# Attention with a gated convolution: one of four probability tiles is turned by TensorE instead of the DMA engines, and a list scheduler orders the work

## The chip, the cores and the metric

The kernel runs on one core of a Trainium2 chip. The metric is the device time of one execution in microseconds (us); less is better. The kernel before takes 1226.25 us, the median of three runs from 1223.54 to 1230.8 us.

## The reference: what is computed

Four batches; q is [4, 12288, 128], kv is [4, 384, 32, 128], all float32.

```python
kv_pool = kv.reshape(B, H // 4, 4, W // 4, 4, C).mean(axis=(2, 4))   # 4x4 blocks: 768 keys
k = v = kv_pool.reshape(B, -1, C) @ w_sr
s = (q @ k.transpose(0, 2, 1)) / sqrt(C)
a = exp(s - s.max(-1));  a /= a.sum(-1) + 1e-9
x = a @ v                                    # [B, 12288, 128]
gate_pre[t] = sum over k of conv_w[k] * x[t - 4 + k]                 # five taps, causal
out = (sigmoid(gate_pre) * (x @ w_val)) @ w_out
```

## The kernel before, in words

The sequence of a batch is cut into 24 groups of 512 queries (`GQ`), 96 groups in all, and a group into four tiles of 128 queries. Channels lie on the partitions for q, x and everything behind x; queries lie on the partitions for the scores.

**Keys.** For each batch kv is summed over 4x4 blocks by VectorE. The first batch comes in 16 pieces by plain loads (`load_kv`, L110). Each later batch comes as eight transfers of whole rows (`load_rows`, L122): the first row of a half is a plain load from the queue of SyncE (SP), the other three are added on the way by accumulating DMAs that GpSimd issues (L128); VectorE then sums groups of four columns (`pool_rows`, L133). TensorE projects the sums by w_sr (L145); the keys are split into a high and a low float32r part (`kh`, `kl`), the values, scaled by a power of two for each channel, into two float16 parts (`vh`, `vl`).

**A tile.** TensorE makes the scores `s` of 128 queries against 768 keys with three products (L251: qh kh, qh kl, ql kh), each of 512 and 256 columns, into one of three double banks of PSUM. VectorE takes the row maximum (L257). ScalarE makes the exponential in place, with the row sum as a by-product (L263), and writes its high float16 half times 2^15 into the buffer `hl` (L282); VectorE writes the low half (L288). So queries still lie on the partitions, and the product with the values wants keys there. For that a DMA transposes the halves of two tiles at a time into `pt` (`p_lo`, L294; 193 issues on SP, the last pair apart).

**A group.** TensorE multiplies `pt` by the values with 18 products of 512 columns into `av` (L303). Meanwhile VectorE adds 1e-9 to the row sums and takes the reciprocal (L270, L271); SP writes the [128, 4] result to DRAM (`rd`, L272) and reads it back as one row on all 128 partitions (`rb`, L277), with the four tiles interleaved. VectorE multiplies `av` by this row into `x` (L322; the row is read with a stride of four elements). ScalarE makes two of the five taps (L330), GpSimd three (L332) and the four additions (L341). ScalarE takes the tanh (L357), TensorE multiplies x by w_val (L361), VectorE combines (L366), TensorE multiplies by w_out (L371), ScalarE copies out (L381), and SP stores two groups at a time (L385). GpSimd also makes the low part of q (L243).

**The order.** Each engine works through its instructions in the order of the program, which is written by hand: one loop over tiles (L442) that places the scores of the next tile, the parts of the product two groups back, and the steps of groups three to five back. Set-up steps of the next batch are dropped in one for each group. The last groups are written out (L502 to L552), with the very last cut into two halves and its convolution on VectorE.

Of the kernel before, what the change touches and what calls it, by code (L numbers as in the profile page):

```python
# [15 lines left out]
R = 4  # L16
P = 128
GQ = 512
NT = GQ // P

# [6 lines left out]
def attn_moe_kernel(ctx, tc, qT, kvT, w_sr, w_moe, outT):  # L27
    """qT, outT: [B, C, N]; kvT: [B, R, C, keys * R]; w_moe: [C, C + C + taps], the columns of
    w_val, w_out and conv_w transposed, as float64 bits (int64) or float32."""
    nc = tc.nc  # L30
    B, C, N = qT.shape
    NK, RR = kvT.shape[3] // R, R * R
# [6 lines left out]
    PIECES = 16  # L39
    AV_CUTS = (0, 6, 9, 12, 18)  # L40
    assert 3 * NCH == AV_CUTS[-1]
    PC = NK // PIECES
    QC = NK // 4
    scale = 1.0 / float(C) ** 0.5

    const = ctx.enter_context(tc.tile_pool(name="const", bufs=1))
    kvp = ctx.enter_context(tc.tile_pool(name="kvp", bufs=4))
    keys = ctx.enter_context(tc.tile_pool(name="keys", bufs=2))
    io = ctx.enter_context(tc.tile_pool(name="io", bufs=2))
    hlp = ctx.enter_context(tc.tile_pool(name="hlp", bufs=3))  # L50
    ptp = ctx.enter_context(tc.tile_pool(name="ptp", bufs=4))
    work = ctx.enter_context(tc.tile_pool(name="work", bufs=2))
    xp = ctx.enter_context(tc.tile_pool(name="xp", bufs=3))
    small = ctx.enter_context(tc.tile_pool(name="small", bufs=6))
    dram = ctx.enter_context(tc.tile_pool(name="dram", bufs=3, space=bass.MemoryType.DRAM))
    ps_s = ctx.enter_context(tc.tile_pool(name="ps_s", bufs=3, space=PSUM))
    ps_av = ctx.enter_context(tc.tile_pool(name="ps_av", bufs=1, space=PSUM))
    ps_m = ctx.enter_context(tc.tile_pool(name="ps_m", bufs=1, space=PSUM))

    def misc():  # L60
        return ps_m.tile([P, GQ], F32, name="m")

    ident = const.tile([P, P], F32, name="ident")
    make_identity(nc, ident)
    wsr = const.tile([C, C], F32, name="wsr")
    wm = const.tile([C, NW], F32, name="wm")
    wval, wout, cwt = wm[:, 0:C], wm[:, C:2 * C], wm[:, 2 * C:]

    def load_moe():
        """Loads the weights; the steps that make float32 of float64's bits, rounded to nearest."""  # L70
        if w_moe.dtype == F32:
            nc.sync.dma_start(out=wm, in_=w_moe)
            return []
        raw = kvp.tile([C, HALF * R], F32, name="rows0", bufs=1).bitcast(I32)[:, :2 * NW]
        rest = kvp.tile([C, HALF * R], F32, name="rows1", bufs=1)
        nc.sync.dma_start(out=raw, in_=w_moe.bitcast(I32))
# [4 lines left out]
        v = nc.vector  # L81

        def two(out, in_, s1, op0, s2, op1):
            return lambda: v.tensor_scalar(out=out, in0=in_, scalar1=s1, scalar2=s2,
                                           op0=op0, op1=op1)

        def one(out, in_, s1, op):
            return lambda: v.tensor_single_scalar(out=out, in_=in_, scalar=s1, op=op)

        def both(out, x, y, op):  # L90
            return lambda: v.tensor_tensor(out=out, in0=x, in1=y, op=op)

        return [
# [14 lines left out]
        ]  # L108

    def load_kv(st, i):  # L110
        t = kvp.tile([C, R, PC * R], F32, name="kvt", bufs=5)
        src = kvT[0].rearrange("r c x -> c r x")
        nc.sync.dma_start(out=t, in_=src[:, :, i * PC * R:(i + 1) * PC * R])
        st["kv", i] = t

    def pool_kv(st, i):
        t = st.pop(("kv", i))
        nc.vector.tensor_reduce(out=st["pool"][:, i * PC:(i + 1) * PC],
                                in_=t.rearrange("c r (k s) -> c k r s", s=R),
                                axis=AX.XY, op=ALU.add)  # L120

    def load_rows(b, st, h, r):  # L122
        src = kvT[b, r, :, h * HALF * R:(h + 1) * HALF * R]
        if r == 0:
            st["rows", h] = kvp.tile([C, HALF * R], F32, name=f"rows{h}", bufs=1)
            nc.sync.dma_start(out=st["rows", h], in_=src)
        else:
            nc.gpsimd.dma_start(out=st["rows", h], in_=src, accum_op=ALU.add)  # L128

    def pool_rows(st, i):  # L130
        t = st["rows", i // 2].rearrange("c (k s) -> c k s", s=R)
        k0 = i % 2 * QC
        nc.vector.tensor_reduce(out=st["pool"][:, i * QC:(i + 1) * QC], in_=t[:, k0:k0 + QC],  # L133
                                axis=AX.X, op=ALU.add)

    def key_tiles(st):
        st["pool"] = keys.tile([C, NK], F32, name="pool", bufs=1)
        for n in ("kh", "kl"):
            st[n] = keys.tile([C, NK], F32R, name=n)
        for n in ("vh", "vl"):  # L140
            st[n] = keys.tile([P, NK], F16, name=n)
        st["vt"] = keys.tile([C, NK], F32, name="vt", bufs=1)

    def project(st, h, m):
        nc.tensor.matmul(m[:, :HALF], wsr, st["pool"][:, h * HALF:(h + 1) * HALF],  # L145
                         start=True, stop=True)
        st["m"] = m[:, :HALF]

    def split_keys(st, h):
        sl = slice(h * HALF, (h + 1) * HALF)  # L150
        m = st.pop("m")

        def high():
            nc.scalar.activation(out=st["kh"][:, sl], in_=m, func=AF.Copy, scale=scale / RR)
            nc.scalar.activation(out=st["vt"][:, sl], in_=m, func=AF.Copy, scale=1.0 / RR)

        def low():
            nc.vector.scalar_tensor_tensor(  # L158
                out=st["kl"][:, sl], in0=m, scalar=scale / RR, in1=st["kh"][:, sl].bitcast(F32),
                op0=ALU.mult, op1=ALU.subtract)  # L160

        return high, low

    def column_scale(st):
        """Steps for the power of two that brings the largest value of each column to
        [2^14, 2^15), on a diagonal, and what takes it and P's 2^15 out again."""
        big = small.tile([C, 1], F32, name="big")
        pw = small.tile([C, 1], F32, name="pw")
        up = small.tile([C, 1], I32, name="up")
        st["down"] = keys.tile([C, 1], F32, name="down")  # L170
        st["diag"] = keys.tile([C, C], F32, name="diag", bufs=1)
        v = nc.vector
        return [
            lambda: v.tensor_reduce(out=big, in_=st["vt"], axis=AX.X, op=ALU.max,
                                    apply_absolute_value=True),
            lambda: v.tensor_single_scalar(out=pw.bitcast(I32), in_=big.bitcast(I32),
# [8 lines left out]
    def values(st, h, m):  # L185
# [4 lines left out]
        st["m"] = m[:, :HALF]  # L190

    def split_values(st, h):
        sl = slice(h * HALF, (h + 1) * HALF)
        m = st.pop("m")

        def high():
# [384 lines left out]
```

## Time and profile before

| | |
|---|---|
| runs | 1223.54, 1230.8, 1226.25 us, median 1226.25 |
| profiled execution: span (its own time) | 1223.5 (1223.54) us |
| mean granted TensorE clock | 0.954 |
| busy: TensorE, VectorE, ScalarE, GpSimd | 84%, 82%, 77%, 67% |
| DMA | 253.19 MB, mean 207 GB/s |
| load of q, of `rb`, landing of a transpose (median) | 5.6, 4.8, 7.0 us |

The profile is of one execution. Busy shares are means over the whole span; a matmul's end is modelled, so TensorE's own pace is read from the starts of its instructions. "Idle before" is the time in which an engine did nothing ahead of the instructions of a group, with what ended it. The share of a DMA queue is that of 16 engines over the span; since two queues overlap, the sum can pass 1.

### The profile page before, as it was taken

The numbers are of one execution on the slowest core, as the hardware profiler recorded it, in microseconds if no ns is written. First come the engines' busy times: TensorE is split into PE (matmuls) and PEld (weight loads), VectorE is DVE, ScalarE is ACT, GpSimd is POOL, SyncE is SP. The second block draws the span as 40 slices with busy tenths as digits, with TensorE's granted clock in tenths as the row PEclk, the third lists the DMA queues.
The fourth block names the chain that finished last, engine by engine and source line by source line (L and its number), as shares of the span: only waits on it lengthen the run. The fifth ranks groups of instructions, "written<-read, shape, count | busy, mean of one in ns | idle before, by whom it ended". The sixth has DMA issues, their size and how long they took to land.

```text
span 1223.5 us, 15077 instructions
## 1 busy us (share of the span) xinstructions
PE 1023.3 (84%) x4502; PEld 622.8 (51%) x4502; DVE 1001.5 (82%) x1251; ACT 940.1 (77%) x1657; POOL 814.2 (67%) x872
## 2 busy tenths in 40 slices
PE   1878886789898789789997878886989999999885
PEld 0644454455564445455555545553555555655552
DVE  5977885799987778699998868776998987988884
ACT  1867785688886778688897768766988988988981
POOL 1165775676785676576777657665867877877871
PEclk9899898899999989899999989898999999999998
DMA  8799999999999999999999999999999999999994
GB/s 251 141 216 203 213 218 167 205 211 201 204 227 227 219 210 214 208 204 212 210 222 225 210 195 226 208 188 194 204 223 207 200 220 213 211 220 212 227 195 116
DMA packets 650321, 253.19 MB, mean 207 GB/s; under 512 B 613632, under 2 KB 622208, under 8 KB 650240
## 3 DMA queue, kind: packets, MB, share of 16 engines
q1 hardware_dynamic: 647648, 238.08, 95.3%
q0 software_dynamic: 2592, 14.16, 7.4%
q8 instruction: 36, 0.59, 0.2%
q14 instruction: 45, 0.37, 0.1%
HBM read 75.83 MB, written 25.36 MB: 83 GB/s over the span
## 4 chain that ended last, share of the span: by engine, by line
DMA 49%; PE 27%; DVE 14%; ACT 5%; issue 3%; SPq 1%; DVEq 0%; ACTq 0%
DMA pt<-hl 47%; PE av L303 13%; PE s L251 7%; DVE nm L257 4%; PE m L361 4%; DVE hl L288 4%; DVE x L322 3%; ACT hl L282 3%; PE m L371 2%; ACT s L263 2%; DVE ze L270 1%; DMA kvt<-in_kv 1%; DVE h L366 1%; DMA rb<-rd 1%; SPq L294 1%
## 5 line engine op out<-in xcount | busy, mean ns | idle before, releaser
L341 POOL TENSOR_TENSOR sum<-sum,tap 128x512 f32<-128x512 f32 x282 | 362.0, 1284 | 330.3 <-ACT tap L330 315.7
L303 PE MATMUL av<-pt,vh 128*128 128x512 f16 x1140 | 400.6, 393 | 106.7 <-DMA pt<-hl 101.5
L288 DVE SCALAR_TENSOR_TENSOR hl<-s,hl 128x768 f16<-128x768 f32 x384 | 365.9, 953 | 113.4 <-ACT hl L282 111.9
L263 ACT ACTIVATE s<-s,nm 128x768 f32<-128x768 f32 x384 | 335.1, 873 | 135.8 <-DVE nm L257 134.8
L282 ACT ACTIVATE hl<-s 128x768 f16<-128x768 f32 x384 | 311.5, 811 | 94.8 <-DMA pt<-hl 83.9
L257 DVE TENSOR_REDUCE nm<-s 128x1 f32<-128x768 f32 x384 | 364.6, 950 | 12.8 <-PE s L251 12.6
L251 PE MATMUL s<-kh,qh 128*128 128x512 f32 (+1 forms) x768 | 280.9, 447 | 45.2 <-DVE hl L288 41.5
L303 PEld LDWEIGHTS <-vh 128*128 128x128 f16 x1164 | 115.8, 99 | 279.1 <-issue 143.0
L303 PE MATMUL av<-pt,vl 128*128 128x512 f16 x570 | 223.3, 392 | 0.0
L251 PEld LDWEIGHTS s<-kh,qh 128*128 128x128 f32 x768 | 142.1, 195 | 136.1 <-issue 91.4
L251 PE MATMUL s<-kl,qh 128*128 128x512 f32 (+1 forms) x768 | 200.6, 343 | 0.0
L251 PE MATMUL s<-kh,ql 128*128 128x512 f32 (+1 forms) x768 | 200.3, 342 | 0.0
L332 POOL TENSOR_SCALAR tap<-x,wm 128x512 f32<-128x512 f32 x282 | 195.6, 747 | 0.2
L243 POOL TENSOR_TENSOR ql<-q,qh 128x512 fp32r<-128x512 f32 x96 | 121.8, 1268 | 53.0 <-ACT qh L239 53.0
L322 DVE SCALAR_TENSOR_TENSOR x<-av,down,rb 128x512 f32<-128x512 f32 x95 | 108.2, 1139 | 48.6 <-PE av L303 28.6
L330 ACT ACTIVATE tap<-x,wm 128x512 f32<-128x512 f32 x188 | 133.9, 713 | 0.0
L251 PEld LDWEIGHTS s<-kl,qh 128*128 128x128 f32 x768 | 120.3, 192 | 18.1 <-DVE kl L158 0.5
L251 PEld LDWEIGHTS s<-kh,ql 128*128 128x128 f32 x768 | 120.4, 192 | 17.1
L341 POOL TENSOR_TENSOR sum<-tap,tap 128x512 f32<-128x512 f32 x94 | 125.2, 1332 | 0.0
L371 PE MATMUL m<-h,wm 128*128 128x512 f32 x188 | 100.1, 614 | 20.8 <-DVE h L366 20.8
L361 PE MATMUL m<-x,wm 128*128 128x512 f32 x188 | 107.1, 654 | 0.0
L303 PEld LDWEIGHTS <-vl 128*128 128x128 f16 x582 | 58.1, 100 | 67.9 <-issue 35.7
(58 smaller groups left out, 638.8 us busy)
## 6 DMA issues: line engine op xcount, KB each, us to landing
rb<-rd SPq DMA_DIRECT2D x96, 256.0 KB, 4.8
q<-in_q SPq DMA_DIRECT2D x47, 512.0 KB, 5.6
out<-o SPq DMA_DIRECT2D x46, 512.0 KB, 3.3
rows<-in_kv POOLq DMA_DIRECT2D x18, 768.0 KB, 9.4
kvt<-in_kv SPq DMA_DIRECT2D x16, 384.0 KB, 5.7
rows<-in_kv SPq DMA_DIRECT2D x6, 768.0 KB, 7.2
pt<-hl SPq DMA_TRANSPOSE x193, 7.0
rd<-r SPq DMA_DIRECT2D x96, 2.0 KB, 2.7
```

Source lines behind the costliest of these rows:

```text
L251: nc.tensor.matmul(s[:, c0:c1], a[:, sl], k[:, c0:c1], start=(i == 0), stop=(i == 2))
L257: nc.vector.tensor_reduce(out=nm, in_=g.s[j], axis=AX.X, op=ALU.max, negate=True)
L263: nc.scalar.activation(out=g.s[j], in_=g.s[j], func=AF.Exp, bias=g.nm.pop(j), accum_out=g.z[:, j:j + 1])
L282: nc.scalar.activation(out=g.hl[:, j % 2, 0], in_=g.s[j], func=AF.Copy, scale=2.0 ** 15)
L288: nc.vector.scalar_tensor_tensor(out=hl[:, j % 2, 1], in0=g.s.pop(j), scalar=2.0 ** 15, in1=hl[:, j % 2, 0], op0=ALU.mult, op1=ALU.subtract)
L303: nc.tensor.matmul(out, g.st[v][:, k * P:(k + 1) * P], g.pt[:, j0:j1, a * NCH + k], start=(i == 0), stop=(i == len(AV_ORDER) - 1))
L322: nc.vector.scalar_tensor_tensor(out=tiles(g.x[:, HALO + c0:HALO + c1]), in0=tiles(av), scalar=g.st["down"], in1=rows, op0=ALU.mult, op1=A ...
L330: nc.scalar.activation(out=g.tap[k], in_=src, func=AF.Copy, scale=w)
L332: eng.tensor_scalar(out=g.tap[k], in0=src, scalar1=w, scalar2=1.0, op0=ALU.mult, op1=ALU.mult)
L341: nc.gpsimd.tensor_tensor(out=s, in0=acc, in1=g.tap[k], op=ALU.add)
L361: nc.tensor.matmul(m, wval, g.x[:, HALO + c0:HALO + c1], start=True, stop=True)
L371: nc.tensor.matmul(m, wout, h, start=True, stop=True)
```

## The change

The hand-written loop is replaced by a planner. Every piece of work is a `Step` with an engine, a duration, a due time, the steps it comes after, and the buffers that it takes and frees. `Plan.order` simulates the five engines, lets the engine that can begin earliest take its ready step with the earliest due time, and the program is emitted in that order; the chip still runs each engine in program order. A group has a period of 10.4 us in the due times (`PERIOD`), its `av` product is due 1.9 periods after its first scores.

Besides the order, these parts differ:

- **Tile 3 of each group** (`TURNED = ((3,),)`) is turned by TensorE: its exponential goes to an SBUF buffer `p`, six blocks of 128 columns are transposed against the identity into a second double bank of PSUM, and the two halves are made from there straight into `pt`. Tiles 0 and 1 go through one DMA transpose, tile 2 through one of its own.
- **Keys** of every batch come in 16 pieces by plain loads on SP, each with a contiguous run in DRAM (the input is laid out anew), and VectorE sums 16 elements at once: 64 loads and 64 sums.
- **1/z**: GpSimd adds 1e-9, VectorE takes the reciprocal and a block transpose of 32x32, four small writes (4 rows of 32 elements each) go to DRAM, and the row comes back with the tiles in order, so `x` reads it contiguously.
- **Taps**: one on ScalarE (was two), four on GpSimd (was three); the sum is made in place in `gate`.
- **Buffers**: four `hl` (was three), three `pt` (was four), four `x` (was three), three q pairs (was two). The PSUM split (three double banks, `av`, `m`) stays.
- **The end**: the last two groups have their convolution on VectorE; the last group is no longer halved.

```diff
-    def load_rows(b, st, h, r):
...
-            nc.gpsimd.dma_start(out=st["rows", h], in_=src, accum_op=ALU.add)
+                nc.sync.dma_start(out=t, in_=kvT[b, i])
+            s = plan.add("SP", 1.05, due(-20 * T + i) if first else at(i) + T, run,
+                         takes=("kvt",), start=at(i))
...
+                v.tensor_reduce(out=st["pool"][:, i * PC:(i + 1) * PC],
+                                in_=ld.tile.rearrange("c (k s) -> c k s", s=RR),
+                                axis=AX.X, op=ALU.add)
...
+        def turned(j, ex):
...
+                    nc.tensor.transpose(state["t"][:, k * P:(k + 1) * P],
+                                        ex.tile[:, k * P:(k + 1) * P], ident)
...
+            flat = lambda a: g.pt[:, j, a * NCH:(a + 1) * NCH].rearrange("p k q -> p (k q)")
+            def hi():
+                nc.scalar.activation(out=flat(0), in_=state["t"][:, :NK], func=AF.Copy,
+                                     scale=2.0 ** 15)
+            def lo():
+                v.scalar_tensor_tensor(out=flat(1), in0=state["t"][:, :NK], scalar=2.0 ** 15,
+                                       in1=flat(0), op0=ALU.mult, op1=ALU.subtract)
...
+                nc.sync.dma_start_transpose(
+                    out=g.pt[:, j0:j0 + width].rearrange("p j k q -> p (j k) q"),
+                    in_=g.hls[j // 2][:, :width].rearrange("p j a k -> p (j a k)"))
...
-        nc.vector.tensor_scalar_add(out=ze, in0=g.z, scalar1=1e-9)
-        nc.vector.reciprocal(out=r, in_=ze)
-        nc.sync.dma_start(out=g.rd, in_=r)
+            nc.gpsimd.tensor_scalar_add(out=g.ze, in0=g.z, scalar1=1e-9)
+            v.reciprocal(out=g.r[:, :NT], in_=g.ze)
+            v.transpose(out=g.rt, in_=g.r)
+                nc.sync.dma_start(out=g.rd[j].rearrange("(b i) -> b i", i=32),
+                                  in_=g.rt[j::32, :])
+            nc.sync.dma_start(out=g.rb, in_=g.rd.rearrange("(o j) p -> o (j p)", o=1)
+                              .broadcast_to([C, GQ]))
...
+            taps = {4: act_tap(4)}
...
+            for k in (1, 2, 3):
+                taps[k] = pool_tap(k)
+            for k in (1, 4, 2, 3):
+                gate = plus(k, taps[k], gate)
...
+    for step in plan.order():
+        step.run()
+AV_DUE = 1.9
+TURNED = ((3,),)
```

## Rows read from the trace of the kernel before

**Rows 1.** The page: busy time (share of the span) and instructions; DMA queues, share of 16 engines.

```profile
PE 1023.3 (84%) x4502; PEld 622.8 (51%) x4502; DVE 1001.5 (82%) x1251; ACT 940.1 (77%) x1657; POOL 814.2 (67%) x872
...
q1 hardware_dynamic: 647648, 238.08, 95.3%
q0 software_dynamic: 2592, 14.16, 7.4%
...
DMA pt<-hl 47%; PE av L303 13%; PE s L251 7%; DVE nm L257 4%; PE m L361 4%; DVE hl L288 4%; DVE x L322 3%; ACT hl L282 3%; PE m L371 2%; ACT s L263 2%; DVE ze L270 1%; DMA kvt<-in_kv 1%; DVE h L366 1%; DMA rb<-rd 1%; SPq L294 1%
```

**Rows 2.** Two stretches, L251 alone: us, PE, PEld busy (records), granted clock, DMA share, GB/s.

```profile
28.00:940.00 912.00, 419.54 (x1764) 294.37 (x1764) 0.95 1.05 207
940.00:1186.00 246.00, 125.27 (x540) 88.42 (x540) 0.98 1.06 213
```

**Rows 3.** Who waited for whom: total us, times, longest us.

```profile
PE av L303 <- DMA pt<-hl: 101.5, 61, 5.5
```

**Rows 4.** Timeline of PE in the last batch: start, us, instructions.

```profile
1000.36 1.02 PE L371 MATMUL m<-h,wm 128*128 128x512 f32 x2
1001.22 0.38 PE L303 MATMUL av<-pt,vh 128*128 128x512 f16 x1
...
1002.95 0.38 PE L303 MATMUL av<-pt,vh 128*128 128x512 f16 x1
...
1003.87 0.52 PE L251 MATMUL s<-kh,ql 128*128 128x512 f32 x2
...
1004.93 0.51 PE L251 MATMUL s<-kh,ql 128*128 128x512 f32 x2
```

**Rows 5.** Stretch of the first key loads: five engines' busy us, clock, DMA share, GB/s.

```profile
10.00:20.00 10.00, 1.65 (x2) 0.50 (x2) 7.23 (x11) 1.49 (x3) 1.26 (x1) 1.00 1.09 332
```

**Rows 6.** Timeline of SP's queue near the end: a pair, a single tile, small issues.

```profile
1169.33 3.64 SPq L294 DMA_TRANSPOSE pt<-hl  x1
1173.06 0.53 SPq L277 DMA_DIRECT2D rb<-rd  x1
1173.68 4.31 SPq L294 DMA_TRANSPOSE pt<-hl  x1
...
1196.99 1.70 SPq L294 DMA_TRANSPOSE pt<-hl  x1
```

**Rows 7.** Timeline around the blocks of L188, f32 by f32.

```profile
39.08 0.75 PEld L188 LDWEIGHTS m<-diag,vt 128*128 128x128 f32 x6
39.19 0.83 PE L188 MATMUL m<-diag,vt 128*128 128x128 f32 x6
...
39.75 0.30 PEld L251 LDWEIGHTS s<-kh,qh 128*128 128x128 f32 x2
```

**Rows 8.** Groups by line: count, busy us, mean ns of one, idle us before and releaser.

```profile
L332 POOL TENSOR_SCALAR tap<-x,wm 128x512 f32<-128x512 f32 x282 | 195.6, 747 | 0.2
...
L330 ACT ACTIVATE tap<-x,wm 128x512 f32<-128x512 f32 x188 | 133.9, 713 | 0.0
...
L322 DVE SCALAR_TENSOR_TENSOR x<-av,down,rb 128x512 f32<-128x512 f32 x95 | 108.2, 1139 | 48.6 <-PE av L303 28.6 <-DMA rb<-rd 18.1 <-POOL sum L341 1.1
...
L270 DVE TENSOR_SCALAR ze<-z 128x4 f32<-128x4 f32 x96 | 88.7, 924 | 0.0
...
L366 DVE SCALAR_TENSOR_TENSOR h<-th,m 128x512 f32<-128x512 f32 x94 | 63.7, 677 | 22.5 <-PE m L361 20.7 <-ACT th L357 1.5 <-issue 0.3
...
L118 DVE TENSOR_REDUCE pool<-kvt 128x48 f32<-128x768 f32 x16 | 15.2, 951 | 8.9 <-DMA kvt<-in_kv 8.7
```

**Rows 9.** DMA issues: count, KB each, median us from issue to landing.

```profile
rd<-r SPq DMA_DIRECT2D x96, 2.0 KB, 2.7
```

**Rows 10.** Timeline: the first and the last scores, and the wait near the end.

```profile
28.14 0.79 PE L251 MATMUL s<-kh,qh 128*128 128x512 f32 x1 [0.58 <-ACT kh L154]
...
1184.07 0.59 PE L251 MATMUL s<-kh,qh 128*128 128x512 f32 x1
...
1200.01 1.11 DVE L322 SCALAR_TENSOR_TENSOR x<-av,down,rb 128x512 f32<-128x512 f32 x1 [8.12 <-DMA rb<-rd]
```

More of the change, by code (lines that the diff above doesn't have):

```diff
@@ L51, in attn_moe_kernel @@
[L51 to L57, printed above, removed]
@@ new lines, in attn_moe_kernel @@
+    pool("th", 2, [C, GQ], F32)
+    pool("h", 2, [C, GQ], F32)
+    pool("o", 3, [C, 2, GQ], F32)
+    pool("nm", 6, [P, 1], F32)
+    for n in ("kh", "kl"):
+        pool(n, 2, [C, NK], F32R)
+    for n in ("vh", "vl"):
+        pool(n, 2, [P, NK], F16)
+    pool("pool", 1, [C, NK], F32)
+    pool("vt", 1, [C, NK], F32)
+    pool("diag", 1, [C, C], F32)
+    pool("down", 2, [C, 1], F32)
+    rows = [sb.tile([P, 32], F32, name=f"r{i}") for i in range(3)]
+    for r in rows:
+        nc.gpsimd.memset(r, 0.0)
@@ new lines, in two, with one, both, weights @@
+    def two(out, in_, s1, op0, s2, op1):
+        return lambda: v.tensor_scalar(out=out, in0=in_, scalar1=s1, scalar2=s2, op0=op0, op1=op1)
+    def one(out, in_, s1, op):
+        return lambda: v.tensor_single_scalar(out=out, in_=in_, scalar=s1, op=op)
+    def both(out, x, y, op):
+        return lambda: v.tensor_tensor(out=out, in0=x, in1=y, op=op)
+    def weights():
+        load_sr = plan.add("SP", 0.3, -50, lambda: nc.sync.dma_start(out=wsr, in_=w_sr))
+        if w_moe.dtype == F32:
+            return load_sr, plan.add("SP", 0.8, 2, lambda: nc.sync.dma_start(out=wm, in_=w_moe))
+        raw = sb.tile([C, 2 * NW], I32, name="raw")
+        rest = sb.tile([C, 5 * NW], F32, name="rest")
@@ L80, in load_moe @@
         low = rest[:, 4 * NW:5 * NW]
[L81 to L93, printed above, removed]
+        runs = [
             two(ex, hi, 20, ALU.logical_shift_right, 0x7FF, ALU.bitwise_and),
@@ L136, in key_tiles @@
[L136 to L147, printed above, removed]
@@ L380, in g_evac @@
[L380 to L389 removed]
+        s = plan.add("SP", 1.0, 2, lambda: nc.sync.dma_start(out=raw, in_=w_moe.bitcast(I32)))
@@ L396, in attn_moe_kernel @@
             g.i, g.b, g.t0, g.st = len(groups), b, i * GQ, states[b]
[L397 removed]
+            g.turned = TURNED[g.i % len(TURNED)]
             groups.append(g)
[L399 to L410 removed]
@@ L540, in attn_moe_kernel @@
-    out_tile(n2)
-    g_evac(n2, n2.m)
-    store(n2)
-    n3.th = g_tanh(n3.gate)
-    h = g_h(n3.th, n3.m)
-    ms = [g_val(n1, bank()[:, :half], *c) for c in cuts]
-    hs = [g_h(th, m) for th, m in zip(ths, ms)]
-    n3.m = g_out(h, misc())
-    g_evac(n3, n3.m)
-    store(n3)
-    for h, c in zip(hs, cuts):
-        g_evac(n1, g_out(h, bank()[:, :half]), *c)
-        store(n1, *c)
+    for b in range(B):
+        setup(b, states[b])
+    for i, g in enumerate(groups):
+        group(g, groups[i - 1] if i else None, groups[i + 1] if i + 1 < G else None)
```

905 lines of the change are left out of this document (535 added, 370 removed).

## The prediction

> **What bounds the kernel now.** I read the busy shares and the queues first, then the pace of the scores in two stretches, then who waits for the transposes, then durations. In the totals no compute engine reaches 85%, but the packets of the hardware queue fill 95.3% of the 16 DMA engines, with 7.4% from the software queue (GpSimd's accumulating loads) on top, and the longest lines of the chain that ended last are transfers `pt<-hl` [rows 1]. So the DMA engines are the suspects. The stretches bear it out. A tile of scores is six matmul records of L251, a group four tiles. Before 940 us, while the next batch's keys are loaded, 1764 records in 912 us make 294 tiles, 3.10 us each, 12.41 us a group; in the last batch 540 make 90 tiles in 246 us, 2.73 us each, 10.93 us a group. The DMA share stands at 1.05 and 1.06 in both [rows 2]: the engines are full, and what differs is what they carry. The waits agree: the largest cause of idle time ahead of TensorE's products is `pt<-hl`, 101.5 us in 61 waits [rows 3].
>
> What must TensorE do in a group? A score tile repeats after 1004.93 - 1003.87 = 1.06 us; eight products `av` take 1002.95 - 1001.22 = 1.73 us, 0.216 each; an output matmul occupies 1001.22 - 1000.36 = 0.86 us [rows 4]. So 4 x 1.06 + 18 x 0.216 + 2 x 0.86 = 9.85 us, and about 0.1 for the set-up of batches. The last batch at 10.93 is thus 9% over its TensorE work, the earlier ones 25%: the change has most to win in the first 72 groups.
>
> **What the change takes off the DMA.** A group of the last batch moves 3 x 0.262 MB of plain data (q, the row of 1/z, the output). Plain loads ran at 332 GB/s [rows 5], so that is 2.37 us, and a transposed pair of tiles costs (10.93 - 2.37) / 2 = 4.28 us. One pair and one single tile instead of two pairs: 1.5 x 4.28 = 6.42. The key loads, 64 of 0.393 MB over 96 groups, add 0.79 at the same rate and replace those that make up the difference of 1.48 us between the two stretches. Sum 9.58 us a group, 1.35 below the DMA work of the last batch and 2.8 below that of the others. That a single tile costs half a pair is borne out on SP: a pair holds it 3.64 us, the one listed single tile 1.70 [rows 6].
>
> **What it puts on TensorE.** Six turned blocks a group. No row shows a transpose. From below: a quarter of an f16 product, 0.054 a block. From above: the blocks of L188, f32 128x128 against f32 128x128, with two weight loads and two matmuls to a block; their six matmuls began at 39.19 and the weights of the next work at 39.75, 0.19 to 0.20 a block. Six of their weight loads take 0.75 us and two take 0.30, so one follows another after 0.11 us [rows 7]. A transpose that loads its block once is nearest to half a block of L188 and can't go below the weight load, so I take 0.12: 0.72 us a group (0.33 to 1.2). TensorE then needs 9.95 + 0.72 = 10.67 us and is the largest load.
>
> The Trainium skill ("TensorE: Matmul & The Clock Gate", Part 4: PE-mode transpose) speaks against this step: about 275 ns for a transpose among other work, and transposes do not count as work that keeps the full clock. No run here shows it yet. By that figure the six blocks are an estimated 1.65 us, and the sum below would be 1203 us.
>
> **The other engines, per group.** ScalarE is busy 940.1 / 96 = 9.79 us [rows 1] and loses one of two taps at 0.71: 9.1. The exponential of the turned tile goes to SBUF instead of PSUM, which no row separates; one instruction of four in a group, it is taken at no change, and even a quarter of a tap either way leaves ScalarE under 9.4. VectorE is busy 1001.5 / 96 = 10.43. The epsilon step goes to GpSimd (-0.92, although a 4-column operation; what made it long stays behind). The final product reads a contiguous row: as `h` with the same operand kinds 0.68 instead of 1.14 (-0.46, at worst nothing). The block transpose lies between 0 and the 0.95 us of a sum over 768 columns and, with 32 columns, is taken at 0.2. Key sums: 64 of 0.95 instead of 28, +0.36. Sum 9.6 [rows 1, 8]. GpSimd has 814.2 / 96 = 8.48, one tap more (+0.75) and the epsilon step (four columns, between 0 and a tap, taken at 0.2), and no longer issues the 18 accumulating loads: at most 9.4 [rows 1, 8]. All lie 10 to 15% under TensorE's 10.67. If that cover goes, each 0.1 us above it is 10 us over 96 groups.
>
> **The queue on SP.** It issues in order. Per group: a pair 3.6 to 4.3, taken at 4.2, a single 1.7 to 2.2, at 1.9; four small writes of 1/z instead of one, and the row: 5 x 0.53, the row's own duration; half a load of q, half a store and two thirds of a key load at 0.53 each: 0.9. Sum 9.7 us [rows 6]. Behind the row's load, which waits for the four writes to land, stand the next transposes and, behind these, the products. The landing of such a write is 2.7 us [rows 9]. I take nothing for this wait, since 1.3 us of slack are there and the next group's transposes can be ordered between; the worst is a rival below.
>
> **The planner's order.** It moves every step, all DMA issues among them. TensorE should meet fewer waits than in the last batch, where the transposes were late. I take 3% idle (0 to 9%, the latter the last batch's): 10.67 x 1.03 = 11.0 us a group. That includes the clock, which stood at 0.98 where TensorE was busiest and at 0.95 elsewhere [rows 2].
>
> **Head and tail.** First scores come at 28.1 us, the last begin at 1184.1 [rows 10], counted to 1186. The head needs the same 6.3 MB and loses the weight conversion between the sums: -2 us (0 to -4). At the end `x` of the last group but one waited 8.12 us for its row, which stood behind two transposes on SP [rows 10]. With the last tile turned by TensorE the queue is free; the split of the last group into halves goes too. I take -8 (0 to -11). What is late next there is TensorE's own products.
>
> **Sum.** 26 + 96 x 11.0 + (1223.5 - 1186 - 8) = 26 + 1056 + 29.5 = 1111.5 us against the profiled execution of 1223.5 (its time 1223.54). The median of the three runs is 2.7 above; so 1114 us. TensorE becomes the bound, and the DMA falls to about 87%.
>
> **Rivals.** First, dear transposes: a block at L188's 0.20, or blocks at the lower of the clock's two levels (1.2 instead of 2.4 GHz), 0.24. TensorE needs 11.15 to 11.4, with 3% idle 11.5 to 11.7, and the sum is 1160 to 1180. For it: f32 data and f32 weights as in L188; whether the clock counts transposes as work shows in no row. Against it: nothing has to be multiplied, and the clock stood at 0.98 in the densest stretch [rows 2]. 0.15. (The Trainium skill's rule above belongs to this case.)
>
> Second, the fixed order wastes as much as the old one in its last batch, 9%: 10.67 x 1.09 = 11.65, and the sum is 1174. For it: three pairs of PSUM banks now serve five holdings a group, and TensorE stands in line when VectorE or ScalarE is late. Against it: the engines that free them have 10 to 15% to spare. 0.14.
>
> Third, slower: SP's line. If the row's load waits out the 2.7 us in each group with nothing issued, SP needs 9.7 + 2.7 = 12.4 us plus the gaps of some 0.06 us between its ten issues, 13.0, and the sum is 26 + 1248 + 29.5 = 1304. It decides against the old kernel from a wait of about 2 us on. For it: SP was already nearly full in the last batch, two pairs of 4.3 and two small issues of 0.53 with half a load and half a store, about 10.2 of 10.93 us [rows 6]. Against it: there the queue was full because the engines behind it were. 0.09.
>
> Fourth, no gain: a single tile's transpose takes the DMA engines as long as a pair; then 2 x 4.28 + 2.37 + 0.79 = 11.72 us, with 3% as above 12.07; with the old head and tail, 28 + 1159 + 37.5 = 1224. The row of 1.70 us speaks against it. 0.05.
>
> **How the numbers follow.** My forecast has 0.57, with its own range 1080 to 1140. With the first two rivals it makes 0.86 for faster; 0.05 for no change (within 0.5%, which is what a measurement of this kernel can tell), 0.09 for slower. The ends of all costs together give 26 + 96 x 10.4 + 29 = 1053 and, with L188's blocks and 9% idle, 1223; both need every cost at one end. I leave these and the third and fourth rival out: 1070 to 1190.
>
> **What would show it.** Right: the pace of scores is near 11.0 us a group in all four batches alike, the DMA share falls below 0.95, `pt<-hl` vanishes from TensorE's waits, and TensorE's busy share is the highest. A turned block repeats every 0.12 us. Wrong: SP waits long at the row's load; TensorE's idle time before scores ends with VectorE's low half; the granted clock falls in the groups.

## The result, and the profile after

The changed kernel takes 1132.53 us (median of four runs, 1131.73 to 1135.18), the kernel before 1227.41 beside it: ratio 0.9237, 95% interval 0.9205 to 0.9269. The forecast was 1114, range 1070 to 1190, that of the likeliest case alone 1080 to 1140. The profiled execution of after has a span of 1131.5 us, its time is 1133.29, its mean granted clock 0.992 (before 0.954).

The page of after: busy time, the hardware queue (packets, MB, share; there is no software queue any more), the chain that ended last by engine and by line. It answers to [rows 1].

```profile
PE 1050.6 (93%) x5056; PEld 667.7 (59%) x5056; DVE 918.4 (81%) x1280; ACT 869.8 (77%) x1559; POOL 884.2 (78%) x1049
...
q1 hardware_dynamic: 488880, 214.49, 86.4%
...
PE 68%; DVE 11%; DMA 9%; SPq 4%; issue 3%; ACT 3%; POOL 1%; DVEq 0%
PE s L445 26%; PE av L610 24%; PE m L705 6%; PE m L714 6%; PE s L532 5%; DMA kvt<-in_kv 4%; DMA rb<-rd 3%; DVE nm L457 3%; SPq L510 2%; DVE hl L498 2%; DVE x L628 2%; DVE pool L266 1%; DVE pt L549 1%; SPq L583 1%; ACT s L471 1%
```

The last two rows follow the work that ended last back from the last instruction (the chain). Landings of DMA transposes, 47% of the chain before, are gone from its lines (2% is SP's issuing of them, `SPq L510`), and TensorE's own work is 68% of it. The scores of after alone (L445, six records a tile, 24 a group) in two stretches, as [rows 2]; the last load of keys is issued at 694.6 us. Columns: us, PE busy (records), granted clock, DMA share, GB/s.

```profile
131.00:731.00 600.00, 288.28 (x1284) 1.00 0.92 201
731.00:1031.00 300.00, 149.98 (x656) 1.00 0.86 179
```

1284 records are 53.5 groups, 11.21 us each; 656 are 27.3, 10.98 us each. Before they were 12.41 and 10.93. The gain lies in the three batches during which keys are loaded, 72 x (12.41 - 11.21) = 86 of the 95 us, and the last batch's pace has hardly moved. Waits of after, as [rows 3, 9]: total us, times, longest.

```profile
PE av L610 <- DMA pt<-hl: 2.4, 3, 1.5
DVE pool L266 <- DMA kvt<-in_kv: 25.8, 18, 3.9
DVE x L628 <- DMA rb<-rd: 8.3, 10, 1.7
SPq L589 <- DMA rd<-rt: 12.2, 12, 3.4
```

TensorE's wait for transposes fell from 101.5 us to 2.4. The row of 1/z, on which the slower rival rested, holds SP for 12.2 us in all, in 12 of 96 groups. The turned block, TensorE's timeline, as [rows 4, 7]: start, us.

```profile
606.46 0.71 PE L532 MATMUL s<-ident,p 128*128 128x128 f32 x5
607.00 0.38 PE L610 MATMUL av<-pt,vl 128*128 128x512 f16 x1
```

Five blocks stand in 607.00 - 606.46 = 0.54 us, 0.108 each, though one record lasts 0.27 us (next fence): the records overlap, and the price is the distance of the starts. Wherever two blocks follow one another in this trace the median distance is 0.109 us. Groups by line of after, as [rows 8]: busy us, mean ns of one, idle before.

```profile
L532 PE MATMUL s<-ident,p 128*128 128x128 f32 x576 | 96.1, 273 | 1.0 <-ACT p L471 1.0
L628 DVE SCALAR_TENSOR_TENSOR x<-av,down,rb 128x512 f32<-128x512 f32 x96 | 71.4, 744 | 9.0 <-DMA rb<-rd 8.3 <-PE av L610 0.3
L445 PE MATMUL s<-kh,qh 128*128 128x512 f32 (+1 forms) x768 | 258.8, 418 | 19.3 <-DVE hl L498 9.6 <-DVE pt L549 7.1 <-DVE r L573 1.2
L498 DVE SCALAR_TENSOR_TENSOR hl<-s,hl 128x768 f16<-128x768 f32 x288 | 271.8, 945 | 13.4 <-ACT hl L487 12.4 <-issue 0.2
L686 POOL TENSOR_TENSOR gate<-gate,tap 128x512 f32<-128x512 f32 x376 | 481.6, 1281 | 14.2
```

The reads of `x` went from 1139 to 744 ns. On SP (as [rows 6]) the 192 transposes, pairs and singles together, last:

```profile
L510 SPq DMA_TRANSPOSE pt<-hl x192: 1285/3298/6100, 40.5 to 1107.9; - x192
```

First and last scores of after start at 31.0 and end at 1101.5 us ([rows 10]: 28.1 and 1186). So the span is 31.0 + 96 x 11.15 + 30.0.

### The profile page after: what moved, and what is told of

It is laid out like the page before. It is cut to its first block, busy times and chain, and to the rows that moved or that the text cites. A ratio compares the mean times of both kernels' runs of the same rounds, so it can differ in the third digit from the quotient of the medians.

```text
span 1131.5 us, 16498 instructions
## 1 busy us (share of the span) xinstructions
PE 1050.6 (93%) x5056; PEld 667.7 (59%) x5056; DVE 918.4 (81%) x1280; ACT 869.8 (77%) x1559; POOL 884.2 (78%) x1049
## 3 DMA queue, kind: packets, MB, share of 16 engines
q1 hardware_dynamic: 488880, 214.49, 86.4%
## 4 chain that ended last, share of the span: by engine, by line
PE 68%; DVE 11%; DMA 9%; SPq 4%; issue 3%; ACT 3%; POOL 1%; DVEq 0%
PE s L445 26%; PE av L610 24%; PE m L705 6%; PE m L714 6%; PE s L532 5%; DMA kvt<-in_kv 4%; DMA rb<-rd 3%; DVE nm L457 3%; SPq L510 2%; DVE hl L498 2%; DVE x L628 2%; DVE pool L266 1%; DVE pt L549 1%; SPq L583 1%; ACT s L471 1%
## 5 line engine op out<-in xcount | busy, mean ns | idle before, releaser
L686 POOL TENSOR_TENSOR gate<-gate,tap 128x512 f32<-128x512 f32 x376 | 481.6, 1281 | 14.2
L610 PE MATMUL av<-pt,vh 128*128 128x512 f16 x1152 | 374.6, 381 | 19.1 <-DVE x L628 11.9
L471 ACT ACTIVATE s<-s,nm 128x768 f32<-128x768 f32 x288 | 251.8, 874 | 111.8 <-DVE nm L457 110.6
L498 DVE SCALAR_TENSOR_TENSOR hl<-s,hl 128x768 f16<-128x768 f32 x288 | 271.8, 945 | 13.4 <-ACT hl L487 12.4
L445 PE MATMUL s<-kh,qh 128*128 128x512 f32 (+1 forms) x768 | 258.8, 418 | 19.3 <-DVE hl L498 9.6
L487 ACT ACTIVATE hl<-s 128x768 f16<-128x768 f32 x288 | 232.9, 811 | 3.8
L445 PE MATMUL s<-kl,qh 128*128 128x512 f32 (+1 forms) x768 | 198.9, 340 | 0.0
L445 PE MATMUL s<-kh,ql 128*128 128x512 f32 (+1 forms) x768 | 197.6, 338 | 0.0
L445 PEld LDWEIGHTS s<-kh,qh 128*128 128x128 f32 x768 | 136.9, 191 | 90.9 <-issue 21.0
L677 POOL TENSOR_SCALAR gate<-x,wm 128x512 f32<-128x512 f32 x94 | 65.4, 696 | 137.7 <-DVE x L628 137.6
L445 PEld LDWEIGHTS s<-kl,qh 128*128 128x128 f32 x768 | 118.8, 190 | 17.4 <-DVE kl L321 0.5
L445 PEld LDWEIGHTS s<-kh,ql 128*128 128x128 f32 x768 | 118.7, 190 | 17.0
L719 ACT ACTIVATE o<-m 128x512 f32<-128x512 f32 x96 | 57.4, 598 | 67.7 <-PE m L714 67.4
L549 DVE SCALAR_TENSOR_TENSOR pt<-s,pt 128x768 f16<-128x768 f32 x96 | 90.9, 947 | 20.1 <-ACT pt L545 19.8
L532 PE MATMUL s<-ident,p 128*128 128x128 f32 x576 | 96.1, 273 | 1.0 <-ACT p L471 1.0
```

The source lines that it names most:

```text
L445: nc.tensor.matmul(t[:, c0:c1], a[:, sl], k[:, c0:c1], start=(n == 0), stop=(n == 2))
L471: nc.scalar.activation(out=out, in_=sc.tile[:, :NK], func=AF.Exp, bias=mx.tile, accum_out=g.z[:, j:j + 1])
L487: nc.scalar.activation(out=g.hls[j // 2][:, half, 0], in_=sc.tile[:, :NK], func=AF.Copy, scale=2.0 ** 15)
L498: v.scalar_tensor_tensor(out=hl[:, half, 1], in0=sc.tile[:, :NK], scalar=2.0 ** 15, in1=hl[:, half, 0], op0=ALU.mult, op1=ALU.subtract)
L532: nc.tensor.transpose(state["t"][:, k * P:(k + 1) * P], ex.tile[:, k * P:(k + 1) * P], ident)
L610: nc.tensor.matmul(g.av, st[name][:, k * P:(k + 1) * P], g.pt[:, :, a * NCH + k], start=(n == 0), stop=(n == len(AV) - 1))
```

## The experiments

Each time is a median; a ratio is to the kernel before on the same occasion. That kernel's own median moved between 1223 and 1236 us from one occasion to another, so differences between occasions of under 1% are read with care. Where an edit changes what the planner is given, the whole order is planned anew; the texts below say where the order is kept.

### What the parts are worth

**Plain key loads alone**, put into the kernel before (`e3_plain_keys`).

```diff
-            nc.gpsimd.dma_start(out=st["rows", h], in_=src, accum_op=ALU.add)
+            nc.sync.dma_start(out=t, in_=kvT[b, i])
```

> The kernel before with one part of the change alone: the keys of batches 1 to 3 come in 16 plain loads on SP, one each group, and VectorE sums 16 pieces, in place of rows that are accumulated by DMA. My theory (the DMA engines are the bound): the difference of 1.48 us between the stretches with and without key loads falls to 0.79 us, so 72 x 0.69 = 50 us less: about 1178 us (1165 to 1195). The rival (the accumulating loads ran beside the rest and cost nothing, the pace differs for another reason, such as the set-up steps): 1227 us, or slower by the 36 sums more on VectorE, up to 1250.

1190.68 us, ratio 0.9753 (0.9697 to 0.9809): within the theory's range, 35 of the 50 us. TensorE's wait for transposes stays, and so does the DMA share (two stretches: us, busy time of PE, PEld, DVE, ACT, POOL, clock, DMA share, GB/s):

```profile
PE av L305 <- DMA pt<-hl: 110.3, 62, 4.2
...
131.00:731.00 600.00, 520.24 (x2321) 318.08 (x2321) 516.85 (x652) 485.68 (x858) 419.30 (x448) 0.97 1.06 218
731.00:1031.00 300.00, 267.97 (x1210) 164.60 (x1209) 260.73 (x331) 252.50 (x447) 219.85 (x234) 0.98 1.05 216
```

This takes work off the DMA engines, the kernel becomes faster, and the DMA engines remain the bound.

**No turned tile, all else as changed** (`e1_no_turn`).

```diff
-TURNED = ((3,),)
+TURNED = ((),)
```

> The changed kernel with no tile turned by TensorE: each group again has two DMA transposes of two tiles, while the planner, the plain key loads, the new 1/z and the taps stay. My theory (the DMA engines set the pace before, TensorE sets it now): a group needs 2 x 4.28 + 2.37 + 0.79 = 11.72 us of DMA in the three batches with key loads and 10.93 in the last, so 72 x 11.72 + 24 x 10.93 + 61 us of head and tail (31 + 30, as measured) = 1167 us, with a few per cent of waits up to 1200. The rival (the planner's order and the lighter steps on VectorE and ScalarE made the gain, the turned tile only costs TensorE time): TensorE needs 9.95 us a group, at the 5% idle of the changed kernel 10.45, so about 1064 us.

1272.74 us, ratio 1.0417 (1.0355 to 1.0478): both theories miss, on the slow side. With all tiles through the DMA the planner's order and the other parts together are slower than the kernel before; between this kernel and the changed one, each in the order planned for it, lie 140 us. Two stretches, as above, and two of TensorE's waits:

```profile
131.00:731.00 600.00, 501.98 (x2186) 299.97 (x2185) 456.52 (x625) 424.87 (x765) 435.03 (x514) 0.96 0.98 210
731.00:1031.00 300.00, 261.12 (x1130) 154.92 (x1127) 212.24 (x295) 212.00 (x382) 226.38 (x268) 0.95 0.93 192
...
PE s L445 <- DVE hl L498: 80.5, 54, 5.7
PE av L610 <- DMA pt<-hl: 8.2, 9, 2.5
```

The DMA share is 0.98 and 0.93, where the order by hand kept it at 1.06: the DMA engines are nearly full again, and the plan lets them idle. TensorE waits little for transposes (8.2 us) and ten times as long for low halves, so how much of the 140 us is DMA work and how much is this plan is not shown. Without the turned tile the other parts are no source of a gain; the turned tile in the order by hand was not run.

### What sets the pace now

**Two turned tiles** (`e2_turn_two`).

```diff
-TURNED = ((3,),)
+TURNED = ((2, 3),)
```

> Two of four tiles turned by TensorE (tiles 2 and 3), one DMA transpose of a pair left. My theory (TensorE is the bound now): six more blocks of 0.11 us, 0.65 us a group, so 1133 + 96 x 0.65 x 1.05 = about 1198 us (1185 to 1210). The rival (SP's queue, the DMA engines or the waits for them still hold the pace): 2.1 us of DMA less and one issue less in each group, so 1133 us or faster, down to 1110.

1367.49 us, ratio 1.12 (1.1126 to 1.1273). Again both miss by far. Its scores in the first stretch, and their waits:

```profile
131.00:731.00 600.00, 230.33 (x1055) 0.99 0.57 140
```

```profile
PEld s L445 <- DVE pt L549: 69.2, 69, 2.4
PE s L445 <- DVE pt L549: 55.6, 74, 2.0
PE s L445 <- DVE hl L498: 50.2, 73, 3.4
```

1055 records are 13.65 us a group. The DMA share is down to 0.57, no engine is full (TensorE, the busiest, has 85% of the span), and scores wait for low halves, the last readers of a PSUM double bank. A turned tile holds a double bank twice, for its scores and for its transposed blocks. That made a new theory: the three double banks, serving six holdings a group here and five in the changed kernel, set or share in the pace.

**Fewer products, planned anew** (`e4_15_products`): 15 of 18 value products.

```diff
-    AV = [(n, k, a) for k in range(NCH) for n, a in (("vh", 0), ("vl", 0), ("vh", 1))]
+    AV = [(n, k, a) for k in range(NCH) for n, a in (("vh", 0), ("vl", 0), ("vh", 1))
+          if n == "vh" or k < 3]
```

> The changed kernel with 15 instead of 18 products of the probabilities with the values in each group (the low part of the values is left out for half of the keys), everything else as it is. My theory (TensorE is the bound): 3 x 0.216 = 0.65 us less a group on TensorE, 9.95 left, still above VectorE's 9.6 and the DMA's 9.6, so 96 x 0.65 = 62 us less, about 1071 us, up to 1090 if the next loads begin to bite. The rival (waits between engines set the pace, TensorE only looks busy): 1120 to 1133 us.

1155.49 us, ratio 0.9464 (0.9407 to 0.952): slower than with all 18. The order changed with the plan, so this run can't tell work from order. The next two keep every instruction's place.

**Three products not issued, same order** (`f1_three_less`).

```diff
+                if name == "vl" and k >= 3:
+                    return
                 nc.tensor.matmul(g.av, st[name][:, k * P:(k + 1) * P], ...
```

> The order of the changed kernel is kept instruction by instruction; only three of the 18 value products of each group (the low halves of the values for the last three blocks of keys) are not issued, so the output lacks them. TensorE has 3 x 0.216 = 0.65 us less in a group. Theory A (TensorE's own work sets the pace of the changed kernel, and the rest is idle time that stays as it is): 96 x 0.65 = 62 us less, 1133 -> 1070 us, accepted between 1060 and 1085. Theory B (the fixed order with its waits sets the pace; TensorE's work fills the time between waits): the time stays, 1115 to 1135 us. Between the two the saving is divided by 62 to give the share of the loop in which TensorE is the bound.

**Each turned block twice, same order** (`f2_turned_twice`).

```diff
+                    for _ in range(2):
                         nc.tensor.transpose(state["t"][:, k * P:(k + 1) * P], ...
```

> The order of the changed kernel is kept; each of the six transposes by TensorE is issued twice into the same place, so TensorE gets 6 x 0.108 = 0.65 us more in a group and nothing else changes. Theory A (TensorE bound, a transpose costs 0.108 us where it stands): +62 us, 1195 us, accepted between 1180 and 1205. Theory B (waits set the pace and have room): 1133 to 1145 us. Rival on the price (a transpose costs what its record lasts, 0.27 us): +157 us, 1290 us.

Three less: 1128.83 us, ratio 0.9209 (0.9136 to 0.9282), 4 us of the 62. These are the three products that the run before left out, so the two kernels have the same work, and the order alone is worth the 27 us between 1155.49 and 1128.83. A difference of that size between two kernels that were planned each for itself can't be put down to their work. Each twice: 1172.54 us, ratio 0.9567 (0.9502 to 0.9632), 40 us of the 62. So 0.65 us more on TensorE costs two thirds of itself, and 0.65 us less gives back 6%: TensorE is at the bound, but a second limit lies right beneath it. In the run with less work, TensorE's busy time, the stretches of its scores and its idle time ahead of them:

```profile
PE 1014.8 (90%) x4768; PEld 635.0 (56%) x4768; DVE 916.1 (81%) x1280; ACT 867.6 (77%) x1559; POOL 882.6 (78%) x1049
...
131.00:731.00 600.00, 278.96 (x1265) 0.99 0.91 200
731.00:1031.00 300.00, 151.78 (x670) 1.00 0.89 183
...
L445 PE MATMUL s<-kh,qh 128*128 128x512 f32 (+1 forms) x768 | 249.4, 406 | 40.0 <-DVE hl L498 24.4 <-DVE pt L549 11.1 <-DVE rt L577 0.7
```

The waits for the two kinds of low half grew from 9.6 + 7.1 to 24.4 + 11.1 us, the same ones as with two turned tiles. They are the largest growth that TensorE's waits name, 19 us of some 28; its busy time on the page fell by 36 us, not by 62. So the double banks are the best named part of the second limit, and the rest of it stays open. The stretches add where it lies: 1265 records are 11.38 us a group (11.21 in the changed kernel), 670 are 10.75 (10.98). With key loads running, less work on TensorE gained nothing.

**Exponentials in SBUF** free the double bank early; the order is planned anew. With two turned tiles (`f3_two_exp_sbuf`) and with one (`f4_exp_sbuf`):

```diff
-                    out = sc.tile[:, :NK]
+                s.tile = out = tile_of(s, "p")
...
+                         frees=[(mx, "nm"), (sc, "s")])
...
-            s_lo = plan.add("DVE", 0.865, ..., lo, [s_hi], frees=[(sc, "s")])
+            s_lo = plan.add("DVE", 0.865, ..., lo, [s_hi], frees=[(ex, "p")])
```

> Two of four tiles are turned by TensorE, as in the kernel that took 1367 us, but the exponential of every tile is written to one of five buffers in SBUF, and the high and low halves are made from there; a score's double bank in PSUM is free as soon as the exponential has read it. Theory S (with two turned tiles the three double banks, which then serve six holdings in a group, set the pace of 13.6 us): the pace falls to TensorE's work of 11.3 us a group plus some 5% idle, 11.9 us, so 31 + 96 x 11.9 + 30 = 1203 us, accepted between 1170 and 1250. Rival (the longer chain through ScalarE and VectorE, exponential, transpose, high half, low half, sets it, and is as long as before): above 1320 us.

> The changed kernel with one tile turned, but the exponential of every tile written to one of four buffers in SBUF and the halves made from there, so that a score's double bank is free some 2 us sooner. Theory S (the 5% of idle time on TensorE are waits for a free double bank): the pace falls from 11.15 to 10.6 to 10.85 us a group, 31 + 96 x 10.75 + 30 = 1093 us, accepted between 1075 and 1110. Rival (the exponential and the halves cost more from and to SBUF, VectorE's low half above all where GpSimd works beside it, or the pace is set by loads from memory): 1130 to 1165 us.

With two turned tiles 1260.51 us, ratio 1.0281 (1.0213 to 1.0349): 107 us less than in PSUM, nearly half of the 235 us that the second turned tile had cost, and just outside the theory's range. With one turned tile 1214.38, ratio 0.9937 (0.991 to 0.9964): 82 us worse, the way of the rival and beyond its 1165. Its groups by line, its chain by engine, and the additions of the changed kernel and of this one (ns, shortest/median/longest):

```profile
L682 POOL TENSOR_TENSOR gate<-gate,tap 128x512 f32<-128x512 f32 x376 | 552.4, 1469 | 16.1
L494 DVE SCALAR_TENSOR_TENSOR hl<-p,hl 128x768 f16<-128x768 f32 x288 | 381.2, 1329 | 39.8 <-ACT hl L483 39.3
...
POOL 51%; DVE 18%; PE 10%; issue 9%; ACT 9%; DMA 2%; SPq 0%; POOLq 0%; DVEq 0%; ACTq 0%
...
L686 POOL TENSOR_TENSOR gate<-gate,tap x376: 1260/1282/1309, 66.2 to 1109.8; 128x512 f32<-128x512 f32 x188
L682 POOL TENSOR_TENSOR gate<-gate,tap x376: 1258/1283/2117, 64.7 to 1192.6; 128x512 f32<-128x512 f32 x188
```

The low half now reads two operands from SBUF and takes 1329 ns instead of 945; GpSimd's additions, unchanged, take 1469 instead of 1281. Half of the additions take no longer than before; the longest went from 1309 to 2117. GpSimd, 51% of the chain, is now the largest part of what sets the time. The Trainium skill ("SBUF — State Buffer", SBUF: two separate sides) states why two such instructions meet: a VectorE instruction with two SBUF inputs and a GpSimd instruction that reads SBUF want the same pair of ports, and the second waits for the whole of the first. The lengthening on both sides, and that some instructions show it and others not at all, agree with it.

**The same with GpSimd relieved** (`g1_exp_sbuf_two_taps`) asks whether GpSimd was the bound there. One tap more goes to ScalarE, the planner gets the measured durations, and the order is planned anew.

```diff
-            taps = {4: act_tap(4)}
+            taps = {k: act_tap(k) for k in (3, 4)}
```

> The kernel with all exponentials in SBUF (1214 us; there GpSimd's additions took 1469 ns instead of 1281, VectorE's low halves 1329 instead of 945, and GpSimd was 51% of the chain of waits), with one more of the five taps given from GpSimd to ScalarE, and the planner's durations of GpSimd and of the low half set to the measured ones. GpSimd's work falls from 11.1 to 4 x 1.47 + 1.5 + 3 x 0.8 + 0.4 = 10.2 us a group; VectorE has 10.65, ScalarE 9.8, TensorE 10.7. Theory G (GpSimd, slowed by VectorE's reading two operands from SBUF, was the bound, and the sooner freed double banks do help): pace 11.0 to 11.2, 31 + 96 x 11.1 + 30 = 1127 us, accepted between 1105 and 1145. Rival (the dearer low halves lengthen the chain of each tile, whoever makes the taps): above 1175 us.

1146.08 us, ratio 0.9316 (0.9244 to 0.9389), 1 us past the theory's range. 68 of the 82 us come back, which fits GpSimd as the bound there, though the order changed with it. But the page and VectorE's low half show what it ran into:

```profile
PE 1056.4 (92%) x5056; PEld 663.9 (58%) x5056; DVE 1047.5 (92%) x1280; ACT 932.3 (82%) x1653; POOL 997.7 (87%) x955
...
L498 DVE SCALAR_TENSOR_TENSOR hl<-p,hl 128x768 f16<-128x768 f32 x288 | 410.7, 1428 | 8.0 <-ACT hl L487 6.6 <-ACT o L720 0.2
```

VectorE is now as full as TensorE, and the kernel is 14 us above the changed one, so no gain from the freed banks is seen.

### The 18 us of the forecast's miss

**No key loads for the later batches, same order** (`g4_no_later_keys`).

```diff
+                if not first:
+                    s.tile = still
+                    return
                 t = tile_of(s, "kvt")
```

> The order of the changed kernel is kept; the 48 loads of key pieces for the second to fourth batch are not issued, and VectorE's sums for them read one constant piece loaded at the start, so the output of the later batches is that of other keys. VectorE, ScalarE and TensorE have all their work. The changed kernel ran at 11.21 us a group between 131 and 731 us, where such loads run, and at 10.98 between 731 and 1031. Theory L (the loads, by VectorE's waits for pieces, 26 us in all, and by the traffic that they put beside the transposes, make that difference): 72 x 0.23 = 17 us less, 1115 us, accepted between 1105 and 1122. Rival (the set-up work itself on VectorE, ScalarE and TensorE, or the fixed order, makes it; the loads are hidden): 1125 to 1136 us.

1111.57 us, ratio 0.9032 (0.8978 to 0.9087); 21 us less than the changed kernel, all its compute kept (the later batches' outputs belong to other keys). The stretches of scores:

```profile
131.00:731.00 600.00, 293.13 (x1305) 1.00 0.85 180
731.00:1031.00 300.00, 152.69 (x667) 1.00 0.86 182
```

The DMA share of the first stretch is 0.85 instead of 0.92; its 1305 records of scores make 11.03 us a group against 11.21. Over 72 groups that is 13 of the 21 us. The second stretch, with no key load in either kernel, moved as well, 10.98 to 10.79, which no load explains (the changed kernel issues its last at 694.6 us); the two kernels ran on different occasions.

**Keys first at the start, sums a period later in the loop** (`h1_keys_first`), and **with one more tile's exponential in SBUF** (`h2_keys_first_one_aside`). Both are planned anew.

```diff
+        s = plan.add("SP", 1.0, 2, lambda: nc.sync.dma_start(out=raw, in_=w_moe.bitcast(I32)), start=20)
...
+            s = plan.add("DVE", 0.35, 1.5 * T, run, [s], start=32.0)
...
-            ... takes=("q",), start=t0 - 5 * T)
+            ... takes=("q",), start=max(t0 - 5 * T, 20 if g.i else 6.0))
...
-                         frees=[(ld, "kvt")], start=at(i))
+                         frees=[(ld, "kvt")], start=at(i) if first else at(i) + 1 * T)
+ASIDE = (2,)        # the second kernel only
```

> The changed kernel with the key pieces of the first batch loaded ahead of the weights and of all but the first pair of queries, the conversion of the weights begun after the first scores, and, in the later batches, each sum over a piece planned one period after its load instead of the moment it is expected. Theory (the 5 us that the start was longer than predicted are VectorE's wait for pieces queued behind other loads and the conversion put among the sums; the loop's key loads cost in part by such waits): first score at 25 to 27 us instead of 31, and 5 to 10 us from the 18 waits for pieces in the loop, together 1115 to 1127 us, 1120. Rival (the loads cost by their traffic beside the transposes, which stays, and the new order gives back at the first groups what the head gains): first score sooner, but 1127 to 1140 us.

> As the kernel with the keys first, but the exponential of tile 2, the last straight one, goes to SBUF and its halves are made from there, so that one more double bank is free early; GpSimd's and VectorE's durations in the planner are set to a third of the way to the slowed ones. By a third of what the kernel with all exponentials in SBUF showed, GpSimd has 9.2 + 0.6 = 9.8 us a group, VectorE 9.6 + 0.4 = 10.0, both under the pace. Theory (a double bank freed early is worth something as long as neither GpSimd nor VectorE becomes the bound): 0.1 to 0.2 us a group less, 10 to 20 us under the kernel with the keys first, 1100 to 1115. Rival (the slowed low half and additions cost as much as the bank gives): within 6 us of the kernel with the keys first, or above it.

The first: 1123.45 us, ratio 0.9158 (0.9111 to 0.9204), the fastest version that does all the work; its runs (1122.15 to 1129.6) lie under all of the changed kernel's. Starts of the first scores, then VectorE's sums over pieces, then the stretches of scores:

```profile
L445 PE MATMUL s<-kh,qh x12: 281/416/796, 24.3 to 38.5; 128*128 128x512 f32 x6, 128*128 128x256 f32 x6
...
L266 DVE TENSOR_REDUCE pool<-kvt 128x48 f32<-128x768 f32 x64 | 59.7, 941 | 6.5 <-DMA kvt<-in_kv 6.4
...
131.00:731.00 600.00, 290.35 (x1279) 0.99 0.93 201
731.00:1031.00 300.00, 151.73 (x660) 1.00 0.88 179
```

Scores begin at 24.3 instead of 31.0 us. VectorE's wait for pieces is 6.4 us instead of 25.8, all of it in the first 36 us; between 131 and 731 us it was 15.5 us in the changed kernel and is none here. Yet the pace with loads is 11.26 us: taking those waits away gained nothing. Of the 9 us the head gives 6.7; the rest is within the spread. That leaves, for what the loads cost, the transfers themselves: their traffic, or their place in SP's queue. These two were not separated.

The second: 1130.87 us, ratio 0.9215 (0.9164 to 0.9266), 7 us above the first; the theory's 1100 to 1115 is out. Its groups by line and its chain:

```profile
L498 DVE SCALAR_TENSOR_TENSOR hl<-p,hl 128x768 f16<-128x768 f32 x96 | 107.8, 1123 | 1.3 <-ACT hl L487 1.0
L678 POOL TENSOR_SCALAR tap<-x,wm 128x512 f32<-128x512 f32 x282 | 229.2, 827 | 0.5
...
PE 45%; POOL 18%; DVE 13%; DMA 10%; ACT 6%; issue 6%; SPq 1%; DVEq 0%; POOLq 0%; ACTq 0%
```

The low half of tile 2 takes 1123 ns instead of 945, GpSimd's taps 827 instead of 697, and GpSimd is 18% of the chain instead of 1%. That is what the rival said, at a third of the dose; that it accounts for the 7 us is not shown, since a new order alone can move as much.

## Why the prediction was right, and where its sizes were off

**The bound.** The DMA engines bounded the kernel before: taking nothing but key work off them gave 1190.68 with their share still at 1.05 to 1.06. After the change TensorE waits 2.4 us for transposes, and it is TensorE's work that sets the time when it grows. The turned tile is needed for the gain, since without it everything else gives 1272.74; how much of it the planner's order adds is not shown. In the last batch nothing was gained (10.93, now 10.98): there TensorE's work and waits come to what the DMA engines took before. The DMA's share, forecast at about 87%, is 86.4%, but that match is luck: the forecast's 9.58 us a group was set against 11.0 us of the loop, while 86.4% of the whole span of 1131.5 us is 10.18 us a group, 6% more DMA time than the sum had.

**The turned block.** Taken at 0.12 us, it measures 0.108. That settles the first rival against itself: neither L188's 0.20 nor the lower clock appeared; the granted clock was 1.00 from 131 us to 1031, with six transposes in every group among the other products. The Trainium skill's figure ("TensorE: Matmul & The Clock Gate", Part 4: PE-mode transpose), about 275 ns, is what a record lasts here (273); issued behind one another the blocks cost 0.108, and the estimate of 1203 us that hung on it fails. Whether transposes count as work for the clock, which the prediction left open, no run here can test, since TensorE had other work all around them. Doubling the blocks cost 40 us, where 0.27 us each would have cost 157.

**The other engines.** Busy time over 96 groups: VectorE 9.57 us (forecast 9.6), ScalarE 9.06 (9.1), GpSimd 9.21 (at most 9.4). The row of 1/z didn't stop SP: the third rival needed 2.7 us in each group and got 0.13. Single transposes do not cost as pairs: the fourth rival's 11.72 us of DMA work a group is more than the pace of 11.21 with loads, where the share was 0.92. It is out.

**The pace** was forecast at 11.0 us a group, "alike" in all batches: TensorE's 10.67 and 3% idle. It is 11.15, and 11.21 against 10.98 in the two stretches. This is the step that was mis-sized, by 96 x 0.15 = 14.4 us: the sum charged the key loads to the DMA engines, to VectorE's sums and to SP's queue, each of which it kept under TensorE's work, and nothing to TensorE's pace. Without the loads the kernel takes 1111.57; with a first score at 31.5 us and the same tail that leaves 96 x 10.94, and TensorE's work with the measured block is 9.95 + 6 x 0.108 = 10.60, so my 3% is what remains without them. No row gave the 3%, so that it fits is partly luck. That the loads cost is shown, by what path (traffic or queue) is not, and the share of the 21 us that lies outside their stretch stays open.

**The second rival**, double banks that serve five holdings, was half right. It gives the changed kernel no 9%, but a limit lies just beneath TensorE (three products less gained 4 us of 62), and the waits for the banks are the ones that grew the most there. The sign that the prediction named for it, TensorE's idle time before scores ending with VectorE's low half, is there in small: 16.7 of 19.3 us. With six holdings the pace is 13.65 us a group, and nearly half of the loss came back when the banks were freed early. That the banks alone make the limit of the changed kernel is not shown.

**Head and tail.** The tail is 30.0 us (forecast 29.5). The head is 31.0 where I said 26: I took the weights' conversion as gone from among the sums, but the chain of after (start us, us) begins with a key piece, the load of the weights and the first step of their conversion (the last row: its idle time before):

```profile
1.66 6.11 DMA kvt<-in_kv
7.78 7.67 DMA raw<-in_w_moe
15.47 1.32 DVE rest L202
...
L202 DVE TENSOR_SCALAR rest<-raw 128x261 int32<-128x261 int32 x3 | 1.9, 629 | 3.8 <-DMA raw<-in_w_moe 3.8
```

In VectorE's order the first step of the conversion (L202) stands ahead of the seventh sum, so VectorE was idle for 3.8 us until the weights landed, and most of the other steps lie between the sums that follow; the later pieces were issued behind the weights and queries. In that order lay the 5 us: with the keys first and the conversion later, scores begin at 24.3. All three misses, 5 us of head, 14.4 of pace and 0.5 of tail, go the same way, so the forecast did not come near by errors that cancel.

## What to carry to other kernels

When work moves from a full engine to one with room, price it by the distance of starts in the receiving engine's timeline, and count the buffers that it holds there: the second tile cost 235 us while no engine had over 85% of the span, and nearly half of it came back when the PSUM banks were freed early. To learn whether an engine still sets the pace, take a little off it and add as much, at the same places in the order: 0.65 us less gave 4 us, 0.65 us more cost 40, which no busy share of 93% could tell. Keep the order while doing it: the same three products less, planned anew, made the kernel 23 us slower instead of 4 us faster. And before an operand is moved from PSUM to SBUF to free a bank, ask who else reads SBUF: here GpSimd's and VectorE's instructions both grew longer, and the kernel 82 us slower.

## What the runs showed of the hardware

- An f32 transpose of 128x128 on TensorE has a record of 273 ns and follows the last after 0.108 us; 576 of them, and 1152 in the kernels with two tiles or with each block twice, left the granted clock at 0.99 to 1.00 between 131 and 1031 us, with the other products among them.
- A VectorE subtraction over 768 columns with one operand in PSUM takes 945 ns, with both in SBUF 1123 to 1428 beside GpSimd's work, and GpSimd's additions grow from 1281 to up to 1469 ns, its taps from 697 to up to 906 (`g1_exp_sbuf_two_taps`).
- The granted clock rose from 0.954 in the kernel before to 0.992, and stood at 0.95 to 0.96 again where no tile was turned and the DMA share was 0.93 to 0.98.
